# An attention and gated-MLP kernel whose instruction order is taken from a timeline model instead of priorities alone

## The chip, the core and the metric

The kernel runs on one core of a Trainium2 chip. The metric is the device time of one execution in microseconds; several executions are timed and the median is given. The core has five engines with a queue of instructions each: TensorE (PE: matmuls, and PEld for its weight loads), VectorE (DVE), ScalarE (ACT), GpSimd (POOL) and SyncE (SP), which here only issues DMAs. Each engine takes its instructions in the order in which they stand in its queue and waits on semaphores for the others.

## The reference

The input x has 2048 tokens of 576 columns. Attention has 32 heads of 18 columns; each token attends to 8 tokens at a distance of two (itself, the one two back, and so on).

```python
x = A_x
h = x + _A_ref(_layernorm(x), A_wqkv, A_wo)        # q,k,v = x @ wqkv; softmax over the 8 tokens; @ wo
h2 = h + _B_ref(_layernorm(h), B_w_gate, B_w_up, B_w_down)
...
g = x @ w_gate          # 576 -> 4608
u = x @ w_up
return (sigmoid(g) * u) @ w_down
```

## The kernel before, in words

**Tiling.** The tokens are cut into four blocks of 512 (even and odd tokens, two halves each), the heads into four groups of eight, the 4608 hidden columns into 36 chunks of 128. Every fp32 operand of a matmul is split in two parts by `split` (L104): ScalarE copies it to a rounded "hi" (L105), DVE subtracts to get "lo" (L106), and three products are added up in PSUM.

**Stages.** From 0 to 240 us the blocks are normalized and q, k, v computed group by group; `qkv` (L355) evicts each tile on ScalarE (L362) and writes q (L364), k and v (L367) to DRAM scratch from ScalarE's queue, since attention needs a window over neighbouring tokens. `attention` (L160) loads these windows from SP's queue (L165 to L167) and computes on DVE: products with k (L173), their sums (L176), softmax (L181 to L190, its exp L186 on ScalarE), products with v (L199) and their sums (L204 to L207); for blocks 1 to 3 the result `o` is written to DRAM from POOL's queue (L210, L212). The MLP goes in two passes: pass 0 for the first pair of blocks (240 to 790 us), pass 1 for the second (from 845). Each pass begins with 14 chunks in the plain form (`single`, L597). Then pairs follow: in pass 0, `pair` (L623) computes a chunk for two blocks with fewer products, from operand sums and weight differences (`operands` and `sums`, L261 to L271; weight differences in `weights`, L543 to L546). It uses three PSUM tiles: b1 is filled, copied to SBUF by ScalarE (L628, L638, L645) and filled again three times; DVE adds b2 and b3 (L633, L646, L651). In pass 1 the hidden chunks of the pairs go through a seven-product down projection (`down_seven`, L722; L733, evicted by ScalarE in L739, accumulated by POOL's DMA in L742). In pass 0 the down projection (`down_tile`, L662, matmuls L671) goes into two PSUM tiles `dp`, evicted by ScalarE or DVE (L679, L681) and accumulated to DRAM by POOL's DMA (L687).

**Background work.** While pass 0 runs its plain chunks, `under_first` feeds in attention of block 1, its projection (`proj_scr`, which loads `oj` and others by `paced`, L523, from SP's queue, and transposes in L140 and L144) and its sums. While the pairs run, `under_rest` feeds in attention of blocks 2 and 3. Between the passes, `last_pair` loads operands back (`tw` from `x`, L933), and the projections of blocks 2 and 3 begin.

**What sets the order.** The program is written to the Tile framework, whose scheduler puts every engine's queue in an order. The code gives priorities: `tc.high_priority(HI)` and `(HC)` with HI = 400 and HC = 700 move the instructions inside ahead by that much of program order, and `tc.issue_after` ties one instruction behind another. Pools of tiles with few buffers add waits, and so does space that is used again: the `oj` tiles of block 2's projection lie where the tiles of the attention's pool lay, so their loads wait until the last attention's result has been read out to DRAM. The context is opened at L1164.

## Time and profile before

| what | value |
|---|---|
| median of 3 runs | 1635.3 us (1633.71 to 1636.6) |
| span of the profiled execution | 1628.5 us |
| median less that span | 6.8 us |
| PE busy | 1573.4 us (97%), 8532 matmuls |
| DVE busy | 1265.6 us (78%) |
| ACT busy | 888.6 us (55%) |
| POOL busy | 188.9 us (12%) |
| moved by DMA | 278.23 MB, 171 GB/s |

The profile shows one execution. Its own time is the span, from the first to the last instruction that is recorded; the device time of a run has a few us around it. Busy times of the engines overlap, so they don't add up to the span. A window's row gives, for a stretch of the span, the busy time of each engine with its count of instructions, and the clock that TensorE was granted as a share of full speed. The list of waits gives the time in which an engine stood still, what it was about to do, and which instruction released it. The chain of waits goes back from the last instruction through what released each step.

### The profile page before, as it was taken

The numbers are of one execution on the slowest core, as the hardware profiler recorded it, in microseconds if no ns is written. First come the engines' busy times: TensorE is split into PE (matmuls) and PEld (weight loads), VectorE is DVE, ScalarE is ACT, GpSimd is POOL, SyncE is SP. The second block draws the span as 40 slices with busy tenths as digits, with TensorE's granted clock in tenths as the row PEclk, the third lists the DMA queues.
The fourth block names the chain that finished last, engine by engine and source line by source line (L and its number), as shares of the span: only waits on it lengthen the run. The fifth ranks groups of instructions, "written<-read, shape, count | busy, mean of one in ns | idle before, by whom it ended". The sixth has DMA issues, their size and how long they took to land.

```text
span 1628.5 us, 22454 instructions
## 1 busy us (share of the span) xinstructions
PE 1573.4 (97%) x8532; PEld 1387.9 (85%) x8532; DVE 1265.6 (78%) x1982; ACT 888.6 (55%) x1565; POOL 188.9 (12%) x230
## 2 busy tenths in 40 slices
PE   6799999989999999999989999999999999999998
PEld 6699988778888888888878988888888888888888
DVE  6899898847999999999636677777667777667755
ACT  5423235425556556655534344777667777667761
POOL 2000010010000100100101100112222121211210
PEclk9999999989999999999999999999999999999999
DMA  6545745565665666576685224698888888888883
GB/s 214 184 141 187 264 179 189 156 194 158 194 160 152 168 151 169 160 184 161 171 249 181 100 87 132 141 186 169 177 173 164 184 180 166 181 170 170 189 174 121
DMA packets 77789, 278.23 MB, mean 171 GB/s; under 512 B 8336, under 2 KB 14224, under 8 KB 76784
## 3 DMA queue, kind: packets, MB, share of 16 engines
q0 software_dynamic: 28944, 111.19, 36.1%
q1 hardware_dynamic: 40304, 143.70, 26.7%
q10 hardware_dynamic: 8432, 21.89, 3.5%
q8 instruction: 67, 1.10, 0.3%
q14 instruction: 42, 0.34, 0.1%
HBM read 145.88 MB, written 133.23 MB: 171 GB/s over the span
## 4 chain that ended last, share of the span: by engine, by line
PE 77%; DVE 10%; DMA 8%; issue 2%; ACT 2%; SPq 0%; POOL 0%; ACTq 0%; DVEq 0%; POOLq 0%
PE b L562 39%; PE dp L671 13%; PE dp L733 11%; PE b L569 7%; DMA wg<-in_wmlp_dram 3%; PE acc L151 3%; DVE pr L173 2%; DVE pr L199 2%; DVE lg L176 1%; DMA o<-kw 1%; PE bgp L151 1%; PE b L151 1%; DVE w L106 1%; DMA oj<-o 1%; DMA kw<-k 1%
## 5 line engine op out<-in xcount | busy, mean ns | idle before, releaser
L562 PE MATMUL b<-tl,w 128*128 128x512 f32 x1728 | 446.4, 397 | 3.0 <-ACT w L105 2.1
L562 PEld LDWEIGHTS b<-tl,w 128*128 128x128 f32 x1728 | 313.0, 189 | 64.5 <-ACT w L105 2.9
L562 PE MATMUL b<-th,w 128*128 128x512 f32 x1380 | 362.0, 397 | 4.4 <-DVE s L646 4.3
L562 PEld LDWEIGHTS b<-th,w 128*128 128x128 f32 x1380 | 252.1, 189 | 59.2 <-DVE s L646 9.7
L569 PE MATMUL b<-th,w 128*128 128x512 f32 x576 | 178.1, 390 | 0.0
L105 ACT ACTIVATE w<-wg 128x384 fp32r<-128x384 f32 (+2 forms) x200 | 117.4, 595 | 111.1 <-DMA wg<-in_wmlp_dram 60.1
L106 DVE TENSOR_TENSOR w<-wg,w 128x384 fp32r<-128x384 f32 (+2 forms) x200 | 128.4, 648 | 63.0 <-ACT w L105 59.5
L739 ACT ACTIVATE ev<-dp 128x576 f32<-128x576 f32 x224 | 145.1, 648 | 33.5 <-PE dp L733 30.7
L742 POOL DMA_DIRECT2D h<-ev x128 | 110.6, 864 | 454.7 <-ACT ev L739 438.0
L151 PE MATMUL acc<-qw,th 128*128 128x432 f32 x512 | 156.8, 368 | 4.3 <-ACT th L105 4.3
L106 DVE TENSOR_TENSOR w<-tw,w 128x512 fp32r<-128x512 f32 x116 | 79.6, 687 | 72.2 <-ACT w L105 71.3
L569 PEld LDWEIGHTS b<-th,w 128*128 128x128 f32 x576 | 108.4, 188 | 23.3
L671 PE MATMUL dp<-d,h1h 128*128 128x288 f32 x640 | 120.5, 297 | 6.5 <-ACT stage L679 6.5
L671 PE MATMUL dp<-d,h0h 128*128 128x288 f32 x640 | 119.2, 296 | 3.0 <-ACT h0h L105 2.1
L105 ACT ACTIVATE w<-tw 128x512 fp32r<-128x512 f32 x116 | 73.2, 631 | 89.4 <-PE b L562 84.1
L671 PEld LDWEIGHTS dp<-d,h1h 128*128 128x128 f32 x640 | 99.4, 190 | 9.7 <-ACT stage L679 6.7
L151 PEld LDWEIGHTS acc<-qw,th 128*128 128x128 f32 x512 | 99.5, 194 | 9.5 <-ACT th L105 4.8
L671 PEld LDWEIGHTS dp<-d,h0h 128*128 128x128 f32 x640 | 99.4, 189 | 7.0 <-ACT h0h L105 2.3
L679 ACT ACTIVATE stage<-dp 128x576 f32<-128x576 f32 x112 | 72.0, 645 | 53.9 <-PE dp L671 42.6
L151 PE MATMUL acc<-qw,tl 128*128 128x432 f32 x256 | 94.4, 369 | 0.0
L362 ACT ACTIVATE ev<-acc 128x432 f32<-128x432 f32 x64 | 33.9, 532 | 106.7 <-PE acc L154 96.2
L173 DVE TENSOR_TENSOR pr<-kw,q 128x1152 f32<-128x1152 f32 x64 | 85.0, 1352 | 7.6 <-DMA kw<-k 7.0
(268 smaller groups left out, 2892.7 us busy)
## 6 DMA issues: line engine op xcount, KB each, us to landing
h<-ev POOLq DMA_DIRECT2D x96, 576.0 KB, 6.8
wg<-in_wmlp_dram SPq DMA_DIRECT2D x49, 928.0 KB, 4.9
h<-stage POOLq DMA_DIRECT2D x28, 1152.0 KB, 10.8
wg<-in_wmlp_dram SPq DMA_DIRECT2D x36, 640.0 KB, 4.8
kw<-k SPq DMA_DIRECT2D x16, 792.0 KB, 4.8
vw<-v SPq DMA_DIRECT2D x16, 792.0 KB, 5.5
wd<-in_wmlp_dram SPq DMA_DIRECT2D x18, 576.0 KB, 6.7
h<-ev POOLq DMA_DIRECT2D x32, 288.0 KB, 6.1
```

Of the source, the lines that this page charges most:

```text
L105: act.activation(hi, src, AF.Copy)
L106: splits.append(dve.tensor_tensor(lo, src, f32(hi), ALU.subtract))
L151: pe.matmul(ps[:, :n], a[:, c, js], m[:, c], start=k == 0, stop=False)
L173: dve.tensor_tensor(pr[:, i], kw[:, j:j + W], q[:, j].unsqueeze(1).broadcast_to([P, W, CG]), ALU.mult)
L362: act.activation(ev[:, :, j], ps[:, :NQ].rearrange("p (t c) -> p t c", t=3), AF.Copy)
L562: pe.matmul(ps, wt[:, a, k0 + c], xx[:, m + c], start=first and k == 0, stop=k == 5, skip_group_check=True)
L569: pe.matmul(ps, wt[:, a, k0], xx[:, 4], start=False, stop=a == 1, skip_group_check=True)
L671: pe.matmul(ps[:, i, :DH2], a[:, js], d[:, m, i * DH2:(i + 1) * DH2], start=k == 0, stop=k == n)
L679: act.activation(hv, ps, AF.Copy)
L733: pe.matmul(ps[:, i, :DH2], a[x][:, js], m[y], start=k in (0, 1, 3) and q == 0, stop=q == 2, skip_group_check=True)
L739: act.activation(hs[:, k % 2], ps[:, :, :DH2], AF.Copy)
L742: pool.dma_start(hsev[:, u, k0:k + 1], hs[:, :k + 1 - k0], accum_op=ALU.add, max_dma_last_dim=8 * D)
```

## The change

One argument is added where the context is opened. With it, the scheduler keeps a clock for each engine in a model of the timeline while it builds the queues, and takes an instruction when the model says that its inputs are ready; without it, priorities and dependencies alone decide. Instructions, tiles, buffers and semaphore rules of the program are the same. The framework's own code isn't part of the kernel.

```diff
-    with tile.TileContext(nc) as tc:
+    with tile.TileContext(nc, schedule_with_timeline_sim=True) as tc:
         tile_attn_glu_kernel(tc, *args)
```

The queues of all five engines come out in another order. TensorE's instructions stand up to 148 places from where they stood, DVE's up to 37, ACT's up to 28, POOL's up to 5, SP's up to 8. Three places follow.

At the start, ScalarE's queue, as a difference: lines with a minus stand there only before the change, lines without a sign in both. `q_0`, `k_0` and `v_0` are the scratch of the first head group, `tok` a block being normalized, `ev` the evicted tile.

```order
 L364 DMA q_0_91<-ev 128x576
-L131 ACTIVATE tok<-h,nm 128x576 x2
-L362 ACTIVATE ev<-acc 128x3x144
-L132 ACTIVATE tok<-tok,rstd 128x576 x2
-L133 ACTIVATE tok<-tok 128x64 x2
-L362 ACTIVATE ev<-acc 128x3x144
-L131 ACTIVATE tok<-h,nm 128x576 x2
-L132 ACTIVATE tok<-tok,rstd 128x576 x2
-L362 ACTIVATE ev<-acc 128x3x144
-L133 ACTIVATE tok<-tok 128x64 x2
 L367 DMA k_0_75<-ev 128x576
 L367 DMA v_0_83<-ev 128x576
```

The writes of k and v now stand directly behind that of q; of the fifteen instructions that stood between, some stand ahead of all three and some behind.

In pass 0, where the plain chunks end and the pairs begin, DVE's queue before. `L681` evicts a down product, `L265`, `L267` and `L269` are operand sums of block 1 (`L263`, the first of them, stands six rows ahead of this piece), `w` and `d` are weight splits.

```order
L265 TENSOR_TENSOR rs_3538<-rs_3537,ar_3535 128x1024
L106 TENSOR_TENSOR h0l<-s,h0h 128x512
L106 TENSOR_TENSOR d<-wg,d 128x576
L106 TENSOR_TENSOR tl<-rs_3538,tl 128x1024
L267 TENSOR_TENSOR ar_3535<-ar_3535,ar 128x1024
L269 TENSOR_TENSOR rs_3539<-ar_3535,rs_3538 128x1024
L681 TENSOR_TENSOR stage<-stage,dp 128x576
```

And after, around the same work:

```order
L681 TENSOR_TENSOR stage<-stage,dp 128x576
L106 TENSOR_TENSOR w_3779<-wg,w_3779 128x640
L106 TENSOR_TENSOR d<-wg,d 128x576
L681 TENSOR_TENSOR stage<-stage,dp 128x576
L263 TENSOR_TENSOR rs_3537<-ar 128x1024
L106 TENSOR_TENSOR d<-wg,d 128x576
L106 TENSOR_TENSOR th<-ar,th 128x1024
L110 TENSOR_TENSOR th<-ar,th 64x512
L106 TENSOR_TENSOR w_3711<-tw,w_3711 128x512
L582 TENSOR_TENSOR s<-s,b_3729 128x512
L106 TENSOR_TENSOR w_3710<-wg,w_3710 128x384
L265 TENSOR_TENSOR rs_3538<-rs_3537,ar_3535 128x1024
```

The sums stood ahead of the first eviction on DVE; now four evictions stand ahead of the first sum, and the pair's own weight splits stand among the sums.

In one of the pairs, TensorE's queue before: `b1` and `b3` are the pair's PSUM tiles, `dp` a down product, `x6` six matmuls in a row.

```order
L671 MATMUL dp_4982<-d_4412,h1h_4693 128x288 x2
L671 MATMUL dp_4982<-d_4412,h1l_4694 128x288 x2
L671 MATMUL dp_4982<-d_4412,h1h_4693 128x288 x2
L562 MATMUL b3_4918<-th_3635,w3_4733 128x512 x6
L569 MATMUL b3_4918<-th_3635,w1_4728 128x512 x2
L562 MATMUL b1_4916<-th_3668,w4_4731 128x512 x6
L569 MATMUL b1_4916<-th_3668,w4_4731 128x512 x2
```

And after, around the same product of b1:

```order
L562 MATMUL b1_4916<-tl_3632,w3_4733 128x512 x6
L569 MATMUL b1_4916<-th_3635,w4_4731 128x512 x2
L562 MATMUL b1_4916<-th_3668,w4_4731 128x512 x6
L569 MATMUL b1_4916<-th_3668,w4_4731 128x512 x2
L562 MATMUL b3_4918<-th_3635,w3_4733 128x512 x6
```

The last product of b1 now stands directly behind the one before it, whose copy to SBUF (L645) lies between the two; before, down products and b3's product stood there.

Between the passes, POOL's queue before, up to the last write of block 3's attention (`o_109`); `h_110` and `h_111` are the accumulated outputs.

```order
L210 DMA o_109<-kw 512x1x144
L687 DMA h_111<-stage 128x2x1152
L687 DMA h_110<-stage 128x2x1152
L687 DMA h_111<-stage 128x2x1152
L210 DMA o_109<-kw 512x1x144
L212 DMA o_109<-kw 512x1x64
L687 DMA h_110<-stage 128x2x1152
L1055 DMA out_dram<-h_110 512x576
```

And after:

```order
L687 DMA h_110<-stage 128x2x1152
L687 DMA h_111<-stage 128x2x1152
L687 DMA h_110<-stage 128x2x1152
L210 DMA o_109<-kw 512x1x144
L212 DMA o_109<-kw 512x1x64
L687 DMA h_111<-stage 128x2x1152
L687 DMA h_110<-stage 128x2x1152
L1055 DMA out_dram<-h_110 512x576
```

Before, one accumulate stood between the last write of `o` and the output's write; now two do: the write has moved ahead of one accumulate.

## The prediction

> **What bounds the kernel now.** I read the page first, then the windows by stage, then TensorE's waits, the chain of waits, and the rows around each wait.
>
> ```profile
> span 1628.5 us, 22454 instructions
> PE 1573.4 (97%) x8532; PEld 1387.9 (85%) x8532; DVE 1265.6 (78%) x1982; ACT 888.6 (55%) x1565; POOL 188.9 (12%) x230
> PE   6799999989999999999989999999999999999998
> DVE  6899898847999999999636677777667777667755
> ```
>
> TensorE is busy for 97% of the span, so only about 55 us (1628.5 - 1573.4) can be won from its idle time. DVE's row says where that can change: at 9 from the eleventh slice to the nineteenth (about 405 to 770 us), 6 or 7 behind it. The windows by stage give both:
>
> ```profile
> 0.00:85.00 85.00, 62.21 (x308) 56.57 (x309) 65.64 (x150) 44.16 (x96) 9.92 (x26) 0.93 0.57 199
> 85.00:240.00 155.00, 152.40 (x818) 144.36 (x818) 142.35 (x176) 43.44 (x91) 5.52 (x7) 0.99 0.53 188
> 240.00:345.00 105.00, 92.33 (x449) 78.01 (x447) 77.25 (x102) 50.04 (x85) 5.87 (x6) 0.90 0.66 205
> 405.00:790.00 385.00, 383.77 (x2095) 337.40 (x2093) 367.32 (x498) 224.58 (x367) 29.96 (x28) 1.00 0.63 165
> 790.00:845.00 55.00, 46.38 (x268) 41.76 (x269) 27.00 (x43) 23.95 (x46) 5.84 (x6) 0.94 0.71 219
> 845.00:1040.00 195.00, 192.81 (x1105) 169.50 (x1104) 134.70 (x246) 83.30 (x152) 16.43 (x21) 1.00 0.42 132
> 1040.00:1560.00 520.00, 519.96 (x2764) 449.93 (x2763) 374.66 (x644) 370.91 (x647) 103.67 (x120) 1.00 0.88 175
> 1560.00:1628.50 68.50, 63.51 (x372) 56.18 (x371) 36.23 (x52) 22.20 (x38) 5.18 (x6) 0.99 0.56 145
> 406.90:722.20 315.30, 315.23 (x1714) 276.82 (x1713) 305.18 (x413) 181.80 (x298) 24.47 (x23) 1.00 0.64 170
> ```
>
> Each row: stretch, length, busy time of PE, PEld, DVE, ACT and POOL with counts, granted clock, DMA share, GB/s. TensorE idles 22.8 us before 85, 12.7 in 240 to 345, 8.6 in 790 to 845; the clock is below 1 in the same three. From 405 to 790 it idles 1.2 us, but DVE has only 17.7 us to spare. TensorE's waits have names:
>
> ```profile
> PE mm L140 <- DVE tok L135: 9.7, 2, 9.1
> PE dp L671 <- ACT stage L679: 6.5, 1, 6.5
> PE b L140 <- DMA oj<-o: 6.2, 1, 6.2
> PE mm L140 <- ACT tok L132: 5.1, 3, 2.6
> PE b L562 <- DVE s L646: 4.3, 2, 3.3
> PE acc L151 <- ACT th L105: 4.3, 1, 4.3
> ```
>
> (total us, times, longest). The first stands at the very start, where the first block must be normalized in any order. The other five sum to 26.4 us, and they hang on where something stands in a queue. The chain shows what lies behind them, and the matmul's pitch:
>
> ```profile
> 35.63 5.72 DMA k<-ev
> 41.41 5.38 DMA kw<-k
> 323.65 2.90 DMA o<-kw
> 327.01 11.27 DMA oj<-o
> 478.36 4.08 PE b L562 x18
> 667.72 3.18 PE dp L671 x24
> 779.96 8.53 DMA tw<-x
> 804.74 10.72 DMA o<-kw
> 816.99 10.16 DMA wg<-in_wmlp_dram
> ```
>
> A 512-column matmul takes 4.08 / 18 = 0.227 us, a 288-column one 3.18 / 24 = 0.132. The matmuls are the same 8532 in the new order, so no work is removed: every gain is a wait that goes, every loss one that comes.
>
> **The change part by part.** My method: for each place I count, in the old and the new order, the instructions between the producer and the user of a result on each engine, times their row's duration. If the producing engine's work is the longer, TensorE waits for at least the difference.
>
> *A, the start.* ScalarE's rows, with an exp that waits at the head of its queue:
>
> ```profile
> 27.47 0.35 ACTq L364 DMA_DIRECT2D q<-ev  x1
> 35.63 0.36 ACTq L367 DMA_DIRECT2D k<-ev  x1
> 61.10 0.42 ACT L186 ACTIVATE lg<-lg 128x256 f32<-128x256 f32 x1 [6.83 <-DVE lg L185]
> ```
>
> The k write is queued 8.2 us behind the q write of the same group, though both read one tile. The new order puts it directly behind. Other work enters ahead of both, so the net gain is less than 8.2: by the count, ScalarE has 4.9 us less ahead of the write. The first attention starts that much earlier, and with it the exp; splits behind that exp are what L151 waits 4.3 us for. Also, two normalizations of block 1 (L132) move up by about 8 us of ScalarE's work, which takes most of the 5.1 us (longest 2.6). I take -6: 4 of the 4.3, 2 of the 5.1. Bounds: both rows whole and 1.6 of the clock (0.93 over 85 us), -11; 0 if the loads of `kw` (5.38) set the start in any case.
>
> *B, 240 to 345.* The transposes (L140) of block 1's projection wait 6.2 us for `oj`, which comes through a write and a load (2.90 + 11.27) after the last attention. In the new order TensorE has 5.4 us more matmuls ahead of them, and the attention ends 1.7 us later on DVE: 6.2 - 5.4 + 1.7 = 2.5 stay, so -3.7. The clock of 0.90 is worth 10.5 us of this stage (0.10 x 105); I credit 1.3 of it to a wait less than half as long. Together -5, from -8 (all of the wait and 1.8 of clock) to 0 (the load ends that much later: 11.27 us for it, against 5.38 for `kw`, says that it shares the DMA engines).
>
> *C, 345 to 790.* Here I expect a loss. DVE's rows for the work that moves in (the sums' row is from 240 to 405 us), and ScalarE's copy of b1:
>
> ```profile
> L199 DVE TENSOR_TENSOR pr<-vw,lg 128x1152 f32<-128x1152 f32 x30 | 39.9, 1353 | 0.4
> L263 DVE TENSOR_TENSOR rs<-ar 128x1024 f32<-128x1024 f32 x1 | 1.2, 1218 | 0.0
> L106 DVE TENSOR_TENSOR w<-tw,w 128x512 fp32r<-128x512 f32 x44 | 30.0, 683 | 0.3
> L645 ACT ACTIVATE s<-b 128x512 f32<-128x512 f32 x22 | 13.1, 596 | 22.4 <-PE b L569 22.4
> ```
>
> Between the same two instructions of DVE (an L681 at 406.9, an L582 at 722.2) the new order has 25 more and 4 fewer. In come the sums of block 1 with their splits (about 12 us at 1.218 and 0.683 each), four L199 pulled ahead (5.4) and smaller ones: 22.9; out go 2.6. DVE's 305.2 us become 325.5. TensorE gets 20 more matmuls between the same points, 3.4 us: 315.2 becomes 318.6. DVE was 10 us shorter than TensorE there; now it is 6.9 longer, and as the first end is fed by TensorE and the last one feeds it, TensorE must wait 6.9 us at least. With one us of DVE's own waits left I take +8. Queued behind a late subtract on DVE are the next pair's sums of s and the operand splits, and TensorE's next product waits for those. In four pairs, b1's last product also stands directly behind the one before, with the copy (0.596) between them; those 2.4 us fall inside DVE's lag, since DVE catches up meanwhile. They are the low end, +2, if results made ahead of need absorb the lag; the high end, +14, keeps 7 of DVE's 10.1 us of idle.
>
> *D, 790 to 845.* SP's queue:
>
> ```profile
> 802.05 0.33 SPq L516 DMA_DIRECT2D wg<-in_wmlp_dram  x1
> 802.44 14.44 SPq L523 DMA_DIRECT2D oj<-o  x3
> 816.99 0.70 SPq L516 DMA_DIRECT2D wg<-in_wmlp_dram  x1
> ```
>
> Three loads of `oj` hold the queue for 14.4 us: their tiles take the space of the attention's pool, and the last attention's `o` is read out of it only from 804.74 to 815.5. The weights behind them land at 827.2, ScalarE's split waits at the head of its queue, the eviction L679 stands behind it, and TensorE waits 6.5. In the new order the last attention has 12 us less of DVE's work ahead and stands 16 us earlier in TensorE's, and its write stands one accumulate earlier on POOL: it lands near 799.5 (815.5 - 16), before SP reaches the loads. The 6.5 go. Of the 3.3 us at L562, which the chain puts behind `tw<-x` (8.53), 2 go: 12.2 us of matmuls then lie between its trigger and the first user, and that load is what is late next. With half a us of clock, -9. Ends: -11.4 (both waits and 1.6 of the clock's 3.3, 0.06 x 55) and -3 (C's lag delays the attention after all).
>
> *E to G.* From 845 to 1040 1.4 us of short waits go and four copies without cover (0.596 each) come, less what DVE hides: +0.5, from -1 to +3. The seven-product pairs keep 0.9 us of cover at their tightest place, before and after: 0, from -1.5 to +4. In the tail two copies lose their cover: +1.5, from 0 to +3.
>
> Sum: -6 - 5 + 8 - 9 + 0.5 + 0 + 1.5 = -10. The span becomes 1618.5; the median of the runs lies 6.8 us above the profiled span (1635.3 - 1628.5), and I keep that: **1625.3 us**, called 1625.
>
> On the clock, one page has a rule against this change. In 240 to 345 and in 790 to 845 the granted clock is 0.90 and 0.94 around waits of 6 us; in 1040 to 1560, where waits are short, it is 1.00. The Trainium skill ("TensorE: Matmul & The Clock Gate", section "A second HAM failure mode: psum-queue depth-cycling") says that short idles between groups of matmuls can already make the clock swing to half and back. The row of 1040 to 1560 speaks against that for waits of a tenth of a us; none here shows it for waits of one.
>
> **The rivals.**
>
> *R1, DVE becomes the bound (slower).* C's 6.9 us count no idle of DVE. In before it idles 10.1 us in that stretch, 17.7 in the stage. Where DVE is the bound, each such us goes into TensorE's time. With all 17.7, C is 6.9 + 17.7 = 24.6, the sum +6.6, the time 1642. The other terms sum to -18, so it is slower from 14.4 us of idle on (6.9 + 14.4 - 18 = +3.3). For: nine slices at 9. Against: part of that idle is DVE waiting for TensorE, and goes when DVE lags. Chance 0.20.
>
> *R2, the transition keeps its wait (same).* The write of `o` takes 10.72 us and the weights 10.16, at a DMA share of 0.71; if C's lag shifts the attention by as much as the order gains, SP still blocks and D is 0: sum -1, 1634. Chance 0.12.
>
> *R3, nothing moves.* The engines meet at the same semaphores and waits change places only: 1635. Against: k's write cannot stay where it was. Chance 0.03.
>
> *R4, C is absorbed.* Only the four copies stay, +2.4 less 2 that DVE's spare time covers: sum -17.6, 1617 to 1618. Chance 0.07.
>
> *R5, the clock.* C's waits come in hundreds of pieces and the clock drops to 0.95 over 315 us: 16 us on top, 1641. This is what that page's rule would do here. Chance 0.04.
>
> **How the numbers follow.** A measurement of this kernel tells about 0.2% (3.3 us) from no change. The forecast (0.54) has half-widths of 5.5, 4, 6, 4, 2, 3 and 1.5 in its terms, about 11 combined in squares: 1614 to 1636. It gives 0.47 faster, 0.05 same, 0.02 slower; R1 0.02 same and 0.18 slower; R2 0.02, 0.09, 0.01; R3 0.03 same; R4 0.07 faster; R5 0.04 slower. Faster 0.56, same 0.19, slower 0.25. The range goes up to R1 and two us below the forecast's own: 1612 to 1642.
>
> **What would show it.** A: the k write within 1 us of the q write, L140 <- L132 nearly gone. B: the wait for `oj` near 2.5 us. C: TensorE short of 7 to 9 us between 390 and 740, in waits for DVE (L106, L582, L646), DVE above 98% there. D: no wait of 6 us at L671 and the three `oj` issues done in about 2 us. I am wrong if DVE's idle there stays above 14 us, or if TensorE still waits over 5 us at L671.

## The result and the profile after

The changed kernel takes 1608.81 us (median of 4 runs, 1607.45 to 1611.02), the kernel before 1635.95 us (4 runs, 1633.71 to 1637.73): a ratio of 0.9834, 95% interval 0.9816 to 0.9852. The forecast of 1625 had the direction, and the time fell below its range of 1612 to 1642. 27 us were won where 10 were expected.

The page of the changed kernel, its span and busy times:

```profile
span 1609.2 us, 22432 instructions
PE 1562.2 (97%) x8532; PEld 1381.6 (86%) x8532; DVE 1253.3 (78%) x1982; ACT 881.9 (55%) x1565; POOL 191.4 (12%) x230
```

The matmuls are the same 8532, TensorE's share stays at 97%. Then the windows by stage, at the same times as before (length, busy time of PE, PEld, DVE, ACT, POOL, granted clock, DMA share, GB/s):

```profile
0.00:85.00 85.00, 69.41 (x344) 63.45 (x345) 71.93 (x154) 43.95 (x98) 10.95 (x26) 0.94 0.59 205
240.00:345.00 105.00, 100.49 (x530) 86.78 (x531) 77.73 (x112) 54.80 (x97) 7.13 (x7) 0.98 0.67 201
405.00:790.00 385.00, 374.36 (x2015) 324.31 (x2013) 357.69 (x485) 215.71 (x356) 31.54 (x30) 1.00 0.62 160
790.00:845.00 55.00, 53.84 (x314) 47.81 (x314) 23.93 (x40) 25.79 (x49) 6.37 (x5) 1.00 0.86 257
1040.00:1560.00 520.00, 520.00 (x2817) 457.01 (x2817) 376.07 (x655) 372.87 (x659) 106.47 (x123) 1.00 0.93 179
```

TensorE's count tells more than its busy time: 344 matmuls instead of 308 up to 85 us, 530 instead of 449 from 240 to 345, 314 instead of 268 from 790 to 845, but 2015 instead of 2095 from 405 to 790. In that stage it now idles 10.6 us (385 - 374.4) where it idled 1.2, and DVE is less busy, not more (357.7 us; 367.3 before). TensorE's waits over the whole span, and those from 380 to 770 us alone (of both lists the rows that the text uses):

```profile
PE mm L140 <- DVE tok L135: 8.7, 1, 8.7
PE b L562 <- DVE s L582: 6.9, 8, 1.9
PE b L562 <- ACT s L645: 5.7, 8, 1.0
PE mm L140 <- DVE tl L106: 4.7, 3, 2.2
PE b L140 <- DMA oj<-o: 1.6, 1, 1.6
PE acc L151 <- ACT th L105: 0.8, 1, 0.8
PE dp L671 <- ACT stage L679: 0.6, 1, 0.6
```

```profile
PE b L562 <- DVE s L582: 4.4, 6, 1.9
PE b L562 <- ACT s L645: 2.7, 4, 0.7
PE dp L671 <- DVE h0l L106: 1.9, 4, 0.6
PE b L562 <- DVE s L646: 1.0, 1, 1.0
PE b L562 <- ACT s L628: 0.9, 4, 0.2
```

The wait of 6.2 us for `oj` is 1.6, the one of 6.5 at L671 is 0.6, the 4.3 at L151 is 0.8, the 5.1 for L132 is gone. New are the waits for L582 and L645 in the pairs, and at the start L140 now waits 4.7 us for L106 where it waited 0.8.

To place them, I add up over all 8532 matmuls the time from one start to the next beyond the pitch of its form (0.227 us for 512 columns, 0.196 for 432, 0.132 for 288, 0.109 for 128). Since the matmuls are the same, the sum can be cut at the same amount of TensorE's work in every kernel. In us lost, by stage (the times are those of before):

```
TensorE's work       start   0-200  200-330 330-400 400-720 720-800 800-950 950-1480 rest   all
ends in before at        9     237      390     461     783     875    1031     1574 1624
before                 9.3    27.9     22.8     1.0     2.0    12.5     5.2     13.3  2.3  96.2
changed                8.8    17.9     10.8     9.1    13.4     2.9     5.4      5.1  3.0  76.6
change                -0.5   -10.0    -12.0    +8.1   +11.4    -9.6    +0.2     -8.2 +0.7 -19.6
```

The two profiled executions differ by 19.3 us (1628.5 - 1609.2); the medians by 27.1. Device time lies 1.7 to 2.4 us above the span in every run whose span is listed, so the profiled execution of before took about 1630.7 (an estimate: its own device time is not listed), 5 us below the median of its kernel, and that of the changed kernel took 1611.02, 2 us above its own. The same sum over the profiles of the runs below shows where the old order varies. The eight profiles that keep its start lose 28 to 31.5 us up to 200 us of work, the eleven with the new start 17 to 19. At the turn (720 to 800), the eight that keep the old order in the pairs and at the turn, leaving aside the one with a short attention, lose 12.4 to 15.5. The profile of before lies at or near the low end in both, so the table shows these two gains at about their least.

### The profile page after: what moved, and what is told of

It reads as the page before. It is cut to its first block, busy times and chain, and to the rows that moved or that the text cites. A ratio compares the mean times of both kernels' runs of the same rounds, so it can differ in the third digit from the quotient of the medians.

```text
span 1609.2 us, 22432 instructions
## 1 busy us (share of the span) xinstructions
PE 1562.2 (97%) x8532; PEld 1381.6 (86%) x8532; DVE 1253.3 (78%) x1982; ACT 881.9 (55%) x1565; POOL 191.4 (12%) x230
## 4 chain that ended last, share of the span: by engine, by line
PE 78%; DVE 12%; ACT 3%; DMA 3%; issue 3%; POOL 0%; SPq 0%; ACTq 0%; DVEq 0%; POOLq 0%
PE b L562 36%; PE dp L733 11%; PE dp L671 11%; PE acc L151 8%; PE b L569 7%; DVE pr L173 2%; DVE pr L199 2%; DVE w L106 1%; DVE lg L176 1%; PE bgp L151 1%; PE b L151 1%; DMA wg<-in_wmlp_dram 1%; DVE pr L204 1%; DVE s L582 1%; PE acc L154 1%
## 5 line engine op out<-in xcount | busy, mean ns | idle before, releaser
L562 PE MATMUL b<-tl,w 128*128 128x512 f32 x1728 | 443.2, 394 | 12.4 <-DVE s L582 6.6
L105 ACT ACTIVATE w<-wg 128x640 fp32r<-128x640 f32 (+2 forms) x200 | 118.6, 597 | 168.4 <-PE b L569 108.7
L106 DVE TENSOR_TENSOR w<-wg,w 128x640 fp32r<-128x640 f32 (+2 forms) x200 | 129.2, 649 | 58.1 <-ACT w L105 55.0
L151 PE MATMUL acc<-qw,th 128*128 128x432 f32 x512 | 156.0, 366 | 0.8 <-ACT th L105 0.8
L739 ACT ACTIVATE ev<-dp 128x576 f32<-128x576 f32 x224 | 141.9, 649 | 24.6 <-PE dp L733 22.4
L671 PE MATMUL dp<-d,h0h 128*128 128x288 f32 x640 | 123.4, 296 | 0.6 <-ACT stage L679 0.6
L671 PE MATMUL dp<-d,h1h 128*128 128x288 f32 x640 | 121.5, 295 | 0.5 <-DVE tail L681 0.5
L106 DVE TENSOR_TENSOR w<-tw,w 128x512 fp32r<-128x512 f32 x116 | 79.5, 686 | 45.4 <-ACT w L105 45.4
L671 PEld LDWEIGHTS dp<-d,h0h 128*128 128x128 f32 x640 | 101.8, 189 | 6.7 <-ACT stage L679 0.9
L671 PEld LDWEIGHTS dp<-d,h1h 128*128 128x128 f32 x640 | 100.6, 188 | 5.5 <-DVE tail L681 0.7
L151 PEld LDWEIGHTS acc<-qw,th 128*128 128x128 f32 x512 | 98.8, 193 | 5.8 <-ACT th L105 1.3
L151 PE MATMUL acc<-qw,tl 128*128 128x432 f32 x256 | 94.5, 369 | 0.4 <-DVE tl L106 0.4
L105 ACT ACTIVATE w<-tw 128x512 fp32r<-128x512 f32 x116 | 73.1, 630 | 30.0 <-PE b L562 23.4
L646 DVE TENSOR_TENSOR s<-s,b 128x512 f32<-128x512 f32 x58 | 39.6, 683 | 59.3 <-ACT s L645 59.3
```

The lines of the kernel that those rows point to most:

```text
L105: act.activation(hi, src, AF.Copy)
L106: splits.append(dve.tensor_tensor(lo, src, f32(hi), ALU.subtract))
L151: pe.matmul(ps[:, :n], a[:, c, js], m[:, c], start=k == 0, stop=False)
L562: pe.matmul(ps, wt[:, a, k0 + c], xx[:, m + c], start=first and k == 0, stop=k == 5, skip_group_check=True)
L646: added[0] = dve.tensor_tensor(s3, s3, b3, ALU.add)
L671: pe.matmul(ps[:, i, :DH2], a[:, js], d[:, m, i * DH2:(i + 1) * DH2], start=k == 0, stop=k == n)
```

## The experiments

In most of them the queues get an order that I choose. The kernel's instructions keep their names from run to run, so a list of names for each engine can be tied together, each instruction behind the one ahead of it on its engine. This is meant to add a place and no wait. Both whole orders were tied this way in a pair of runs below that also shorten one operation: they took 1608.87 and 1634.52 us, about as long as the two kernels themselves.

```diff
+def _queue_order(nc, tc):
+    by = {i.name: i for i in nc.cur_bb.bb.instructions}
+    link = mybir.DependencyInfo(mybir.DependencyClass.NoSync, mybir.DependencyReason.DATA)
+    for row in ORDER:
+        names = [f"I-{n}" for n in row]
+        for a, b in zip(names, names[1:]):
+            tc.add_manual_dep(by[b], a, link, reason="order")
...
         tile_attn_glu_kernel(tc, *args)
+        _queue_order(nc, tc)
```

A stage is what the scheduler had issued, on all engines, between two of TensorE's matmuls. "Old" is the order of before, "new" that of the changed kernel. Each ratio is against the kernel before, run on the same chip.

### One stage at a time

**New order at the start only.**

```diff
-ORDER = old
+ORDER = new for 0 to 240 us, old behind it
```

> The order of before, except that what before issues from 0 to 240 us stands in the changed kernel's order. Theory S: the waits of the start go, 8 to 12 us, 1624 to 1628 us. Rival: TensorE arrives earlier at 240 us and waits there for the first weights and operands instead; 3 us or less are left, 1633 us or more.

1621.94 us, ratio 0.9917 (0.9902 to 0.9931): 13 us, one more than the first theory gave. In the profiles the loss before 240 us falls from 27.9 to 17.2, and no other stage gains. The start is separate, as that theory had it.

**The writes of k and v alone.**

```diff
 L364 DMA q_0_91<-ev 128x576
+L367 DMA k_0_75<-ev 128x576
+L367 DMA v_0_83<-ev 128x576
...
-L367 DMA k_0_75<-ev 128x576
-L367 DMA v_0_83<-ev 128x576
```

> The kernel before, with two DMAs moved on ScalarE's queue: the writes of k and v of the first group of block 0 stand directly behind that of q instead of fifteen instructions later. Theory K (the late write holds up the first attention, and through the exp that waits in ScalarE's queue the splits behind it): the attention starts 5 to 8 us earlier, 4 to 8 us of TensorE's waits between 58 and 85 us go, 1627 to 1631 us. Rival (the order of the normalizations and splits around it makes the gain): 1 us or less, 1634 us.

1630.99 us, ratio 0.9978 (0.9964 to 0.9992): 2 to 4 us (3.6 lost less up to 240 us). ScalarE's row of the write and TensorE's waits up to 240 us, of this kernel:

```profile
27.42 0.44 ACTq L367 DMA_DIRECT2D k<-ev  x1
```

```profile
PE mm L140 <- ACT tok L132: 5.8, 4, 2.9
PE acc L151 <- ACT th L105: 1.9, 1, 1.9
```

The write leaves at 27.4 instead of 35.6 us and the wait behind the exp falls from 4.3 to 1.9, as theory K says. But the waits for L132 stay (5.8): two thirds or more of the start's gain come from the rest of its order. The normalizations that stand earlier and the splits around them are in it; no run takes these apart.

**New order from 240 to 405 us only.**

```diff
-ORDER = old
+ORDER = new for 240 to 405 us, old around it
```

> The order of before, except that what before issues from 240 to 405 us stands in the changed kernel's order; the sums of block 1 stay inside this stage. Theory S: the wait for oj and the slow clock behind it go, 9 to 10 us, 1626 us. Rival W: without putting the sums off the stage gains at most 3 to 5 us, 1631 to 1633 us.

1638.20 us, ratio 1.0017 (1.0006 to 1.0029): no gain, and less than rival W had left. The wait for `oj` shrinks (22.8 lost become 12.8), and at the first pair it all comes back (1.0 become 14.0). TensorE's waits from 380 to 420 us in this kernel:

```profile
PE b L562 <- ACT s L606: 6.1, 1, 6.1
PE b L562 <- DVE s L582: 3.6, 1, 3.6
```

Rival W holds here in its mechanism: the new order reaches `oj` later because it puts the projection and the sums off, and when these have to be done ahead of the pairs, the pairs wait for them (DVE works on the sums and their splits from 396.9 to 410 us).

**New order inside the pairs only.**

```diff
-ORDER = old
+ORDER = new for 405 to 785 us, old around it
```

> The complement: the order of before everywhere, except that what before issues between 405 and 785 us stands in the changed kernel's order among itself; the sums of block 1 stay ahead of the pairs. Theory S: the order inside the pairs is what costs, the loss of 19 us comes whole, 1636 + 19 = 1655 us. Rival W: what costs is the work put off into the pairs (22.9 us of DVE), and that does not come along here; only the copies without cover cost, 5 to 6 us, 1642 us.

1655.44 us, ratio 1.0121 (1.0102 to 1.0139): 20 us slower, with the sums ahead of the pairs as in before. From 400 to 720 us of TensorE's work it loses 13.4 us, the same as the changed kernel. So this loss isn't the work that was put off; the order inside the pairs makes it. From 330 to 400 us, where the changed kernel loses 9.1, this one loses 7.0: there too the sums among the pairs account for about 2 us only.

**Old order inside the pairs only.** Two versions: cut where before starts its pairs (the sums ahead of them), and cut inside the pairs of the changed kernel (the sums stay where the change put them).

```diff
-ORDER = new
+ORDER = old for 405 to 785 us of before, new around it
```

> The queues have the changed order everywhere except in the pairs of pass 0 (405 to 785 us of before), where they have the order of before. Theory S (the places are separate, each gain and loss is made by the order inside its own stage): the pairs lose about 19 us less than in the changed kernel, the rest keeps its gain, 1609 - 19 = 1590 us. Rival W (work is only put off: what TensorE gains from 240 to 405 us is paid back in the pairs, where the sums of block 1 now stand): with the sums back ahead of the pairs, 240 to 405 us loses its 10 us again, about 1600 us.

```diff
-ORDER = new
+ORDER = old for 447 to 749 us of the changed kernel, new around it
```

> The changed kernel, except that what it issues between 447 and 749 us of its own profile, the inside of the pairs of pass 0, stands in the order of before; the sums of block 1 stay where the change put them, across the first pairs. Theory O (inside the pairs the order costs, not the amount of work): 12 us of waits go, 1609 - 12 = 1597 us. Rival V (DVE has too much to do there whatever the order, because of the work put off): at most 3 us, 1606 us.

1618.63 us (0.9899, 0.9884 to 0.9914) and 1615.02 us (0.9880, 0.9863 to 0.9896): both slower than the whole change, against both theories. Inside the old order the waits are gone (the first loses 1.6 us from 400 to 720, the changed kernel 13.4), but the seams between two orders cost: the first loses 14.7 us from 330 to 400, the changed kernel 9.1. At the turn the first loses 13.4, about as much as before (12.5), although the turn has the new order. The second kernel's waits from 440 to 800 us are nearly all at its two seams:

```profile
PE b L562 <- ACT s L645: 6.1, 1, 6.1
PE b L562 <- ACT s L628: 3.1, 1, 3.1
```

**New order at the turn only.**

```diff
-ORDER = old
+ORDER = new for 785 to 845 us, old around it
```

> The order of before, except that what before issues from 785 to 845 us (the turn between the passes) stands in the changed kernel's order. Theory C (the stages from 240 to 850 us are coupled: the waits at the turn went because the attention, moved up in the pairs, was done earlier, and that was paid there): the attention ends as late as before, the waits stay, 0 to -2 us, 1633 us. Rival S (the order of the turn itself removes them): -9 us, 1625 us.

1634.57 us, ratio 0.9992 (0.9980 to 1.0004). The wait at L671 falls from 6.5 to 1.9, and another takes its place (waits from 780 to 860 us of this kernel):

```profile
PE b L151 <- DVE th L110: 6.2, 1, 6.2
PE dp L671 <- ACT stage L679: 1.9, 1, 1.9
```

The gain at the turn needs what comes ahead of it: theory C.

**New order in the seven-product pairs only.**

```diff
-ORDER = old
+ORDER = new for 1040 to 1560 us, old around it
```

> The order of before, except that what before issues from 1040 to 1560 us (the seven-product pairs) stands in the changed kernel's order. Theory S (the order of this stage alone removes the short waits that it had in each pair): 8 us of 1635, 1627 us. Rival: these are hiccups of the memory traffic that came out lower in one execution and do not hang on the order: 1635 us.

1625.87 us, ratio 0.9944 (0.9927 to 0.9961): 7.6 us, and the loss there falls from 13.3 to 5.7. The gain belongs to this stage's order.

**The start and the seven-product pairs together.**

```diff
-ORDER = old
+ORDER = new for 0 to 240 us and for 1040 to 1560 us, old elsewhere
```

> The order of before from 240 to 1040 us, the changed kernel's order at the start (0 to 240) and in the seven-product pairs (1040 to 1560). Theory C (all that the change does from 240 to 1040 us nets to about 2 us): the two parts add up, 12.9 + 7.6 = 20.5 us, 1613.5 us, at most 5 us above the whole change. Rival: the parts need each other (an earlier arrival at 240 us meets later loads), 1620 us or more.

1615.54 us, ratio 0.9875 (0.9853 to 0.9898): 20 us of the 27. The two parts add up (12.9 + 7.6 = 20.5). What the change does between them is worth the rest, 2 us by the profiled executions (38.3 lost from 200 to 800 us of TensorE's work become 36.2) and up to 7 by the medians.

**In the seven-product pairs, TensorE's order old and the others' new.**

```diff
-ORDER[DVE], ORDER[ACT] = old
+ORDER[DVE], ORDER[ACT] = new for 1040 to 1560 us, old elsewhere
```

> The kernel before; from 1040 to 1560 us DVE and ScalarE have the changed kernel's order, TensorE keeps that of before. Theory P (the waits of a tenth of a us come from too little work of TensorE's own between two products that share a PSUM tile): nothing is gained, 1635 us. Rival (they come from late operands of DVE or ScalarE): 8 us, 1627 us.

1764.16 us, ratio 1.0798 (1.0773 to 1.0822), which neither theory had. The waits from 1040 to 1700 us come 15 times each, once in each pair; the two longest:

```profile
PE b L562 <- ACT s L628: 43.4, 15, 2.9
PE dp L733 <- ACT ev L739: 25.7, 15, 1.7
```

Here an order of one engine is good only with the orders of the others. Which engine's order makes the 8 us can't be told by taking it alone, so neither theory is settled; the opposite mixture was not tried.

### What makes the loss in the pairs

**Cover between b1's products.** On TensorE alone, at four places:

```diff
-L671 MATMUL dp_5151<-d_4574,h0h_4856 128x288 x2
-L671 MATMUL dp_5151<-d_4574,h0l_4857 128x288 x2
-L671 MATMUL dp_5151<-d_4574,h0h_4856 128x288 x2
 L562 MATMUL b1_4916<-tl_3632,w3_4733 128x512 x6
 L569 MATMUL b1_4916<-th_3635,w4_4731 128x512 x2
+L671 MATMUL dp_5151<-d_4574,h0h_4856 128x288 x2
+L671 MATMUL dp_5151<-d_4574,h0l_4857 128x288 x2
+L671 MATMUL dp_5151<-d_4574,h0h_4856 128x288 x2
 L562 MATMUL b1_4916<-th_3668,w4_4731 128x512 x6
```

> The changed kernel; on TensorE alone, in the four pairs where b1's last product stands directly behind the one before it, the nearest group of 6 or 8 down products is moved between the two (1.1 us of cover). Theory O: each of the four waits of 0.85 us goes, 3.4 us, 1605.5 us. Rival V, as the prediction had it: these waits lie inside DVE's lag, which takes their place: 1609 us.

1610.81 us, ratio 0.9860 (0.9844 to 0.9876): no change against 0.9834, as rival V had it. The waits for L645 go from four to one, those for L582 grow (from 380 to 770 us of this kernel; 4.4 and 2.7 in the changed one):

```profile
PE b L562 <- DVE s L582: 5.7, 7, 1.9
PE b L562 <- ACT s L645: 1.0, 1, 1.0
```

**The needed operation first.** On DVE alone, at nine places like this one of the changed kernel: the copy s (L645) is there at 534.15, the add that TensorE waits for (L646) stands behind two operations of the attention and ends at 537.25.

```profile
533.91 1.35 DVE L199 TENSOR_TENSOR pr<-vw,lg 128x1152 f32<-128x1152 f32 x1
535.30 1.36 DVE L204 TENSOR_TENSOR pr<-pr 128x1152 f32<-128x1152 f32 x1
536.57 0.68 DVE L646 TENSOR_TENSOR s<-s,b 128x512 f32<-128x512 f32 x1
```

```profile
533.55 0.60 ACT L645 ACTIVATE s<-b 128x512 f32<-128x512 f32 x1 [1.67 <-PE b L569]
```

```profile
537.31 1.65 PE L562 MATMUL b<-th,w 128*128 128x512 f32 x6 [1.00 <-DVE s L646]
```

```diff
-L199 TENSOR_TENSOR pr<-vw,lg 128x1152
-L204 TENSOR_TENSOR pr<-pr 128x2x576
 L646 TENSOR_TENSOR s<-s,b_4918 128x512
+L199 TENSOR_TENSOR pr<-vw,lg 128x1152
+L204 TENSOR_TENSOR pr<-pr 128x2x576
```

> The changed kernel; on DVE alone, at nine places in the pairs where TensorE waits for a subtract or a product of s that stands behind one to three operations of the attention, those operations are moved directly behind it (15 operations in all). Theory O: these nine waits sum to 8.3 us and go, 1601 us. Rival V: DVE's work is the bound, the waits come back at the next products: 2 us or less, 1607 to 1609 us.

1610.03 us, ratio 0.9847 (0.9830 to 0.9864): no change. The nine waits shrink or go, and others come: 1.1 us less are lost from 400 to 720 and 2.2 less from 330 to 400, but 2 to 3 more at the start, from 200 to 330 and at the turn together. By now rival V, too much work for DVE, had the better record, and the next runs were made to show it.

**The attention later.** Three and six of its operations:

```diff
-attention operation k of blocks 2 and 3 at its place k
+attention operation k of blocks 2 and 3 at the place of k + 3
```

> The changed kernel, with the attention of blocks 2 and 3 put three of its own operations later on DVE (each operation stands where the third one after it stood; exp and the writes of o go along): about 4 us of DVE's work leave the pairs and land behind them, where in the changed kernel the last write of o is done some 10 us before SP reaches the loads of oj. Theory V (DVE's amount of work is the bound of the pairs): 4 us less in the pairs, no new wait at the turn, 1605 us. Rival: the pairs are not bound by DVE's amount, 1609 us.

```diff
-attention operation k of blocks 2 and 3 at its place k
+attention operation k of blocks 2 and 3 at the place of k + 6
```

> The same with six operations, about 8 us of DVE's work. Theory V: up to 8 us less in the pairs; the last write of o then comes about when SP reaches the loads of oj, so that 0 to 6 us of the wait at the turn may return: 1601 to 1607 us. Rival: 1609 us or, with the wait at the turn back, 1615 us.

1620.19 us (0.9908, 0.9889 to 0.9928) and 1685.32 us (1.0307, 1.0287 to 1.0327): 11 and 77 us slower than the changed kernel. This says nothing for or against V, since the shift breaks something else. With three operations, it is in part the exp (L186): it stands on ScalarE ahead of copies of b1, and when DVE reaches its input later, a copy waits behind it (two waits of up to 1.9 us for L638). With six operations it is the weights. TensorE's waits from 380 to 900 us there:

```profile
PE b L562 <- ACT s L638: 33.7, 4, 11.5
```

Three of the four, of about 11 us each, make nearly all of it. SP's rows and ScalarE's ahead of the first of these:

```profile
535.43 0.32 SPq L165 DMA_DIRECT2D q<-q  x1
535.86 0.97 SPq L516 DMA_DIRECT2D wg<-in_wmlp_dram  x1
```

```profile
544.49 0.68 ACT L105 ACTIVATE d<-wg 128x576 fp32r<-128x576 f32 x1 [12.03 <-DMA wg<-in_wmlp_dram]
545.08 0.58 ACT L638 ACTIVATE s<-b 128x512 f32<-128x512 f32 x1
```

SP's queue was not shifted. The load of weights leaves only when the attention's load ahead of it has left, and that load now waits longer for its tile. ScalarE's split of the weights waits 12.0 us for them, and the copy stands behind the split. The other two waits have the same rows, with a load of the attention 0.4 us ahead of that of the weights.

**Less work on DVE, the same places.** In both orders the first add over the window, in the attention of blocks 2 and 3, works on 18 of its 144 columns and leaves out the rest:

```diff
+            c = CG if b < 2 else DH
-            dve.tensor_tensor(pr[:, :, 0:4], pr[:, :, 0:4], pr[:, :, 4:8], ALU.add)
+            dve.tensor_tensor(pr[:, :, 0:4, :c], pr[:, :, 0:4, :c], pr[:, :, 4:8, :c], ALU.add)
```

> The changed kernel's order; in the attention of blocks 2 and 3 the first add over the window (L204) works on 18 of its 144 columns only, so 16 operations on DVE take about 0.2 us instead of 1.35, 18 us less of DVE's work, and the attention's result leaves out part of the sum. Theory V (the amount of DVE's work is the bound of the pairs): 12 us of waits there go, 1597 us. Rival O (where its operations stand): only waits directly behind an L204 shrink, 1 to 3 us, 1607 us.

> The order of before with the same cheaper add (it leaves out the same part of the sum). Theory C (in the order of before the same excess of DVE's work shows as a late end of the attention, and so as the waits at the turn): the attention ends up to 18 us earlier, the waits of 3.4 and 6.7 us at the turn go, 1626 us. Rival: the turn's waits come from the DMAs themselves: 1634 us.

1608.87 us (0.9849, 0.9833 to 0.9864) and 1634.52 us (1.0003, 0.9991 to 1.0015): no change in either, and V falls, and C as I had put it with it. The add takes 0.304 us instead of 1.35, 16 times, which is some 17 us less work on DVE. In the changed order 13.4 us lost from 400 to 720 become 11.1. DVE's idle time from 405 to 760 us grows from 17.6 to 28.3 us; the rest of the time won there is filled with work that came into the window. The row of the changed kernel, then that of the kernel with the cheaper add:

```profile
405.00:760.00 355.00, 344.73 (x1850) 298.31 (x1849) 337.39 (x455) 199.14 (x328) 28.79 (x27) 1.00 0.62 161
```

```profile
405.00:760.00 355.00, 346.91 (x1867) 300.04 (x1866) 326.69 (x460) 200.37 (x331) 28.77 (x27) 1.00 0.62 161
```

In the order of before the end of the attention shows why its wait stays (L583 and L208 are L582 and L207 here, one line further down). DVE's rows:

```profile
799.96 0.30 DVE L205 TENSOR_TENSOR pr<-pr 128x144 f32<-128x144 f32 x1
802.22 0.69 DVE L583 TENSOR_TENSOR s<-s,b 128x512 f32<-128x512 f32 x1 [1.95 <-PE b L570]
806.55 0.75 DVE L207 TENSOR_TENSOR pr<-pr 128x576 f32<-128x576 f32 x1
807.89 0.45 DVE L208 TENSOR_TENSOR kw<-pr 128x288 f32<-128x288 f32 x1
```

The add L205 is done at 800.3. The next operations of the attention stand behind an add of the pair that waits for TensorE until 802.2 and six operations that follow it, and `o` is written from 808.64 on. TensorE's wait at L671 is 5.8 us there. DVE's time isn't short; the attention's last operations have their place behind something that waits.

**A short attention, the same places.** In both orders every operation of the attention of blocks 2 and 3 works on one head of eight and leaves out the other seven:

```diff
+        n = HG if b < 2 else 1
+        c = n * DH
...
-                dve.tensor_tensor(pr[:, i], kw[:, j:j + W],
+                dve.tensor_tensor(pr[:, i, :, :c], kw[:, j:j + W, :c],
...
-        act.activation(lg, lg, AF.Exp, scale=SCALE)
+        act.activation(lg[:, :, :, :n], lg[:, :, :, :n], AF.Exp, scale=SCALE)
```

> The changed kernel's order; in blocks 2 and 3 every operation of the attention works on one head of eight only (the other seven heads are left out), so that the 168 operations on DVE become short and some 150 us of DVE's work go. Theory O (places): the nine waits behind attention operations go, 8 us; the four waits of 0.85 us and the five of 0.38 us between a product of b1 and its copy stay, 5 us: 1601 us. Rival L (the pair's own operations on TensorE, ScalarE and DVE stand in lock step): the waits only move, 1607 us or more.

> The order of before with the same short attention. If the place of the attention's last operations, behind adds of the pair that wait for TensorE, sets when o is written: the waits at the turn stay, 1632 to 1635 us. If the time of the operations ahead sets it: the waits of 3.4 and 6.7 us go, 1624 us.

The changed order takes 1600.70 us (0.9790, 0.9776 to 0.9805): 8 us less than with the whole attention, as theory O had it to the us. DVE is busy for 215 of 355 us and TensorE still loses 7.9 us from 400 to 720 us of its work. The window, and the waits from 380 to 850 us (L649 is L645 here, L632 L628):

```profile
405.00:760.00 355.00, 351.27 (x1901) 305.92 (x1901) 215.30 (x470) 201.67 (x337) 27.53 (x26) 1.00 0.62 162
```

```profile
PE b L566 <- ACT s L649: 2.7, 4, 0.7
PE b L566 <- ACT s L632: 0.7, 3, 0.2
PE b L566 <- DVE s L586: 0.2, 1, 0.2
```

What is left are mostly the copies without cover, at the same four places. The waits for s (L582 before, L586 here) went from 4.4 to 0.2. This run shortens every operation of the attention, so alone it doesn't tell their places from their amount; that 17 us less on the adds left the time as it was speaks for the places. In the order of before the short attention takes 1627.31 us (0.9955, 0.9942 to 0.9969), between the two expectations: the wait of 3.3 us for L646 goes, the one of 6.5 stays at 6.2. The wait that goes is less than half of the 8 us; I haven't placed the rest.

```profile
PE dp L675 <- ACT stage L683: 6.2, 1, 6.2
```

As I read it, that one is set by a place, the other one by the time of what stands ahead.

## Why the prediction was right in direction and wrong in size

**A, the start (-6 forecast, -10.5 found).** The size is within its bounds by the profiles (13 by the medians of the run with the new start is beyond them), and the mechanism is half right. I gave the write of k two thirds of the gain; alone it is the smaller part (2 to 4 us). I credited only 2 of the 5.1 us of waits for L132; the new order takes them all, though L140 then waits 3.9 us more for L106.

**B, 240 to 345 (-5 forecast, -12 found).** Outside the bounds. The wait for `oj` came out about as forecast (2.5 forecast, 1.6 found). The term that was mis-sized is the 1.3 us of clock: the granted clock rose from 0.90 to 0.98, 8.4 us of 105. In before it is at one half from 244.3 to 251.2, 305.8 to 309.2 and 333.1 to 343.3 us; only the last of these stands at the wait for `oj`, the others follow waits for splits (L105, L106) that the new order shortens too. In the changed kernel one such stretch of 3.4 us is left. And I had booked the gain as final. The run with this stage's order alone shows that it can be a loan: where the work put off has to be done ahead of the pairs, all of it is lost again. In the changed kernel the sums stand among the pairs, and there they cost about 2 us.

**C, the pairs (+8 forecast, +19.5 found).** The step that failed is "DVE was 10 us shorter than TensorE there; now it is 6.9 longer", and "TensorE must wait 6.9 us at least" with it. Such a count between two points holds for one path through the queues; read as the stage's bound it was wrong, since the order alone costs the same 13.4 us with the sums moved back, and some 17 us less work on DVE take only 2.3 us off it and leave the time as it was. Also failed: "those 2.4 us fall inside DVE's lag". The four waits at b1 took 0.85 us each in the changed kernel, and they stay when the attention is short. What the runs show in its place: about 8 us go when the attention's operations are short, and about 5 stay, at copies without cover. In the trace nine waits, 8.3 us in all, stand where an operation of the attention is on DVE directly ahead of the one that TensorE waits for. That these places make the 8 us is the reading that is left with V gone, not a thing shown alone: either part moves elsewhere when it is mended by hand at single places.

**D, the turn (-9 forecast, -9.6 found).** Right in size. The reason was half right: the turn's own order gains nothing, the attention must end earlier. But not because DVE has 12 us less ahead: with some 17 us less the wait stayed (5.8 us), and with the short attention too (6.2). The rows say that its last operations have another place; no run moved them alone.

**E and G (+0.5 and +1.5 forecast, +0.2 and +0.7 found).** Right in size; no run tests the reasons.

**F, the seven-product pairs (0 forecast, -8.2 found).** The step that failed is "0.9 us of cover at their tightest place, before and after". The minimum of cover was the same and what it covered wasn't: before, 0.9 us (seven down products) stood against an add on DVE (0.69), now against a copy on ScalarE (0.60). A second place has eleven down products, 1.46 us, against a copy and then an add (0.60 and 0.69); now it has twelve. In before a product starts 0.05 us behind the add at both (DVE's rows at 1081 and 1086 us, TensorE's at 1081):

```profile
1081.07 0.69 DVE L646 TENSOR_TENSOR s<-s,b 128x512 f32<-128x512 f32 x1 [1.84 <-ACT s L645]
1085.92 0.69 DVE L985 TENSOR_TENSOR r<-s,b 128x512 f32<-128x512 f32 x1
```

```profile
1081.57 0.29 PE L733 MATMUL dp<-d,s2l 128*128 128x288 f32 x1
1081.81 0.50 PE L562 MATMUL b<-th,w 128*128 128x512 f32 x1
```

From 1081.57 to 1081.81 are 0.24 us for a pitch of 0.132. Five pieces of 0.05 to 0.11 us, about half a us in all, stand in each of 15 pairs, and none in the changed kernel. Three of the five, each of 0.11 us, stand at these two starts or one matmul behind them; for the other two I show no cause, and no run takes the five apart. I had seen them and taken them for noise that stays; they were too short for the list of waits.

**The sum.** -10 against -19.6 between the profiled executions: A, B and F were 4, 7 and 8 us better, C 11 worse. Another 7 us came from a misreading: I took 6.8 us between median and span for a constant of the measurement. It is about 2, and the rest was that the profiled execution of before was shorter than most.

**The rivals.** R1's price for the pairs (24.6) was nearer than mine, but its mechanism, DVE as the bound, is refuted, and the sum stayed far on the other side. R2 and R3 did not come. R4 was the nearest in time, for another reason. R5's clock did not come: from 405 to 790 us the granted clock is 1.00 in spite of some twenty waits, most of 0.4 to 1.2 us. Only behind the longest, 2.0 us at 425, a slower stretch shows, 3.4 us at one half:

```profile
427.70:431.10 3.40, 3.40 (x11) 2.86 (x10) 3.40 (x7) 1.23 (x2) 0.00 (x0) 0.50 0.74 266
```

The rule of the Trainium skill ("TensorE: Matmul & The Clock Gate", section "A second HAM failure mode: psum-queue depth-cycling") speaks of short idles that come often. The trace doesn't agree with it for this kernel's waits of up to 1.2 us, with the clock at 1.00 from 431 to 790 us; a single wait of two us is not the case that it tells of.

## What to carry to other kernels

With queues that are worked off in order, look for what stands directly ahead of an instruction that the busiest engine waits for, not only for how much work an engine has: some 17 us less of DVE's work changed nothing, and moving the attention by three of its own operations cost 11 us. Mending single places by hand gained nothing here either. A gain in one stage that comes from putting work off must be followed to where the work is done; cut the sum at equal work of the busiest engine and compare stage by stage. And before a short repeated wait is written off, multiply it: about half a us in each of 15 pairs was most of 8 us here.

## What the runs showed of the hardware that I had not expected

Device time lies 1.7 to 2.4 us above the span in all runs; executions of the kernel before spread over 8 us (1631.04 to 1639.13 in one series of 19). A single TensorE wait of 2.0 us was followed by 3.4 us at half the clock (427.7 to 431.1 us), while waits up to 1.2 us left it at 1.00. And orders of engines that don't belong together are dear: 130 us over 15 pairs (1764.16 against 1633.38), 8.7 us for each.
